# Score subtraction and exponential moved to the end of their own unit, and the last value product as one sum group

## The chip, the cores and the metric

The kernel runs on one core of a Trainium2 chip. The metric is the device time of one execution in microseconds (us); lower is better. Five runs of the kernel before the change stand behind its median, and one further run was taken with the hardware profiler.

## The reference

Two decode-attention blocks, A and B, each take one query token for 4 batch entries. Queries are `x @ wq` with 32 heads of 128, four query heads share one of 8 key/value heads, and the two results are concatenated:

```python
q = (x @ wq).reshape(B, 1, 32, 128).transpose(0, 2, 1, 3)
scores = einsum("bhqd,bhkd->bhqk", q, repeat(k, 4)) * 128 ** -0.5
o = einsum("bhqk,bhkd->bhqd", softmax(scores), repeat(v, 4))
out = o.reshape(B, 1, 4096) @ wo
```

Block A uses all 8192 keys of its cache; block B uses only the last 2048. Everything is bf16 at the interface. Nearly all bytes are keys and values: the profile counts 184.56 MB read.

## The kernel before, in words

**Units.** The work is cut into 20 units `u` of equal size (4 MB of keys, 4 MB of values). Units 0 to 3 are block B, one per batch entry with all 8 key/value heads; units 4 to 19 are block A, one per batch entry and pair of key/value heads. `L` is the last unit, 19. A unit has `NT` = 128 tiles of 128 keys. Two consecutive units make a *turn*; TensorE (PE) runs the ten turns as a hardware loop (`nc.Fori`), the other engines run straight code. Every engine's order is written out by hand: `op` and `add` append to one list per engine, and waits are named semaphore events such as `("exp", u)`.

**One unit on PE.** Sixteen jobs `T` transpose keys, eight tiles at a time, into one of four PSUM banks `KTB` (line 256). VectorE (DVE) copies the even jobs to SBUF (`ev[k]`, line 264), ScalarE (ACT) the odd ones (line 265). Three jobs later PE multiplies them with the queries (`pe_S`, line 289) into `SA[u % 2]` (first half of the scores) and `SB` (second half). Behind the sixteenth transpose, PE works on the unit before: `pe_SM(u-1)` sums its probabilities with a matrix of ones (line 315) and eight chunks `pe_PV(u-1, c)` of 16 matmuls multiply them with the values (line 303) into `OTB`, as `NSEG` = 4 sum groups of 32 tiles each. For block A the four groups are added later.

**One unit on the other engines.** At the end of unit `u`, DVE takes the maximum of the second half of its scores (`dve_max`, line 395; the first half's came earlier), joins the halves (`dve_maxc`), adds a mask (`dve_addmask`), and GpSimd (POOL) reduces the maximum over the partitions (`pool_ar1`, line 416, result `MB`). DVE then does the sum and reciprocal of unit `u-1` (`dve_sum`, `dve_rcp`) and `add_norm(u-1)`, which for block A adds the four groups (`OS`, line 469) and multiplies by the reciprocal (line 472). Only inside unit `u+1` does it treat unit `u`'s scores: after `ev[0]` the mask is taken off the maximum (`dve_submask`, line 423) and the first half of the scores is subtracted (`dve_sub`, line 433), after `ev[2]` the second half; ACT does the exponential (`act_exp`, line 442) after `ev[3]`, from `Dt` into `PT`.

**Output projection.** In the first unit of each turn three small jobs (`OT`, `OL`, `OPJ`) project the finished heads of one group; `OPJ` (line 366) needs a 1 MB piece of the output weight in `Wo_sb`. The last group is projected after the loop from `Wl_sb` (line 660).

**After the loop.** DVE and ACT do subtraction and exponential of unit `L`, PE seeds the two output banks (`pe_seed`, line 642), sums (`pe_SM(L)`), multiplies the eight value chunks into `KTB[0]`, whose loads arrive in four pieces (`VL`), and after `add_norm(L)` multiplies with the last weights; two copies and two small stores end the kernel.

**Loads.** All large loads are issued by SyncE (SP) in one order: keys of `u`, values of `u-1`, keys of `u+1`, and so on, with two buffers each. Keys of `u` wait for the last transpose of `u-2`, values of `u` for the last value product of `u-2`. The pieces of `Wo_sb` stand in the same queue, one per turn from turn 3 on.

Of the kernel before, what the change touches and what calls it, by code (L numbers as in the profile page):

```python
# [14 lines left out]
def bass_concat_heads__gqa_block_cached__sliding_block_cached__decode_kernel(  # L15
# [22 lines left out]
    NT = SK // 64  # L38
    NSEG = 4
    TS = NT // NSEG  # L40
    C = 2 * REP
# [9 lines left out]
    NW = 64  # L51
# [11 lines left out]
    L = NU - 1  # L63
# [6 lines left out]
    with ExitStack() as es:  # L70
# [30 lines left out]
        RL = sb("RL", [128, 4, NSEG * C], F32)  # L101
# [6 lines left out]
        PT = sb("PT", [128, 2, NT * C + NW], BF16)  # L108
        OT_sb = sb("OT_sb", [128, 2, NSEG, C, Bn], BF16)
# [21 lines left out]
        tjob_idx, qp_idx, xt_idx, perm_idx, ot_idx, ol_idx, opj_idx = {}, {}, {}, {}, {}, {}, {}  # L131
# [28 lines left out]
        def add(d):  # L160
            op(d["eng"], d["fn"], waits=d["waits"], inc=d["inc"])
# [132 lines left out]
        def pe_PV(u, c, bank=None, waits=()):  # L294
            otb = bank if bank is not None else OTB
            slot = u % 2

            def fn(pe):
                ins = None
                for i in range(TC):  # L300
                    t = c * TC + i
                    s, j = t // TS, t % TS
                    ins = pe.matmul(out=otb[:, s * NW:(s + 1) * NW], lhsT=V_sb[:, slot, t, :],  # L303
                                    rhs=PT[:, slot, t * C:t * C + NW], start=(j == 0), stop=(j == TS - 1))
                return ins
            op("pe", fn, waits=waits, inc=("PV", u * NC + c))

        def pe_SM(u):
            def fn(pe):
                ins = None  # L310
                for s in range(NSEG):
                    n = TS * C // NW
                    for i in range(n):
                        c0 = s * TS * C + i * NW
                        ins = pe.matmul(out=SA[u % 2][:, s * NW:(s + 1) * NW], lhsT=onesb[:, :], rhs=PT[:, u % 2, c0:c0 + NW],  # L315
                                        start=(i == 0), stop=(i == n - 1))
                return ins
            op("pe", fn, waits=[("exp", u) if u >= 0 else None], inc=("SM", u))
# [63 lines left out]
        def ncol(u):  # L382
            return NSEG * C if units[u]["P"] == 1 else C
# [35 lines left out]
        def dve_submask(u):  # L419
            n, P = ncol(u), units[u]["P"]  # L420

            def fn(dve):
                return dve.tensor_tensor(out=MBm[:, 0:n], in0=MB[:, 0:n], in1=MASK[P][:, 0:n], op=AluOpType.subtract)
            return dict(eng="dve", fn=fn, waits=[("ar1", u)], inc=("pm", u, 1))

        def dve_sub(u, h):
            S, n = nseg(u), ncol(u)
            Sh = max(1, S // 2)
            m0 = h * Sh * C if S > 1 else 0
            bank = SA[u % 2] if h == 0 else SB  # L430

            def fn(dve):
                return dve.tensor_tensor(  # L433
                    out=Dt[:, h * NTH * C:(h + 1) * NTH * C].rearrange("p (s j h) -> p s j h", s=Sh, h=C),
                    in0=bank[:, :].rearrange("p (s j h) -> p s j h", s=Sh, h=C),
                    in1=MBm[:, m0:m0 + Sh * C].rearrange("p (s o h) -> p s o h", o=1, h=C).broadcast_to([128, Sh, NTH // Sh, C]),
                    op=AluOpType.subtract)
            return dict(eng="dve", fn=fn, waits=[("pm", u, 1)], inc=("sub", u, h))

        def act_exp(u):  # L440
            def fn(act):
                return act.activation(out=PT[:, u % 2, 0:NT * C], in_=Dt[:, :], func=ACTF.Exp, scale=scale)  # L442
            return dict(eng="act", fn=fn, waits=[("sub", u, 1)] + ([("PV", (u - 2) * NC + NC - 1)] if u else []), inc=("exp", u))
# [10 lines left out]
        def dve_rcp(u):  # L454
            n = ncol(u)
            return dict(eng="dve", fn=lambda dve: dve.reciprocal(out=RL[:, u % 4, 0:n], in_=LB[:, 0:n]), waits=[("sum", u)], inc=("rcp", u))

        def add_norm(u, bank=None):
            un = units[u]
            P, b = un["P"], un["b"]  # L460
            otb = bank if bank is not None else OTB
            last = ("PV", u * NC + NC - 1)
            if P == 1:
                add(dict(eng="dve", fn=lambda dve: dve.tensor_tensor(
                    out=OT_sb[:, 1, :, :, b], in0=otb[:, 0:NSEG * NW].rearrange("p (g w) -> p g w", g=NSEG)[:, :, 0:C],
                    in1=RL[:, u % 4, :].rearrange("p (g c) -> p g c", g=NSEG), op=AluOpType.mult),
                    waits=[last, ("rcp", u)], inc=("otr", u)))
                return
            add(dict(eng="dve", fn=lambda dve: dve.tensor_reduce(
                out=OS[:, :], in_=otb[:, 0:NSEG * NW].rearrange("p (g w) -> p w g", g=NSEG)[:, 0:C, :], axis=AX.X, op=AluOpType.add),  # L470
                waits=[last] + ([("otr", u - 1)]), inc=("os", u)))
            add(dict(eng="dve", fn=lambda dve: dve.tensor_tensor(
                out=OT_sb[:, 0, un["gp"], :, b], in0=OS[:, :], in1=RL[:, u % 4, 0:C], op=AluOpType.mult),
                waits=[("os", u), ("rcp", u)], inc=("otr", u)))

        def dve_otp(tn):
            P, q = pieces.get(tn, (1, 0))
            w = [("pset",)]
            if tn in pieces:
                w.append(("otr", Bn - 1 if P == 1 else Bn + q * Bn + Bn - 1))  # L480
            if tn:
                w.append(("T", ot_idx[tn - 1]))
            return dict(eng="dve", fn=lambda dve: dve.tensor_copy(out=OTp[:, :, :], in_=OT_sb[:, P, q, :, :]), waits=w, inc=("otp", tn))

        def pool_setup0(pool):
# [87 lines left out]
        for u in range(NU):  # L573
            turn[0] = tn = u // 2
            odd = u % 2 == 0
            ev = {}
            extra = {}
            otp = dve_otp(tn) if odd else None
            at = -1

            def anchored(d):
                extra.setdefault(at, []).append(d)
            for tok in TOK:
                if tok[0] == "T":
                    ev[tok[1]] = pe_T(u, tok[1])
                    if tok[1] % 2 == 0:
                        at = tok[1]
                elif tok[0] == "S":
                    pe_S(u, tok[1])
                elif tok[0] == "SM":  # L590
                    pe_SM(u - 1)
                else:
                    pe_PV(u - 1, tok[1], waits=[("V", u - 1) if u >= 1 else None] if tok[1] == 0 else [])
                if odd and tok in AFTER:
                    kind = AFTER[tok][0]
                    anchored({"OT": pe_job_OT, "OL": pe_job_OL, "OPJ": pe_job_OPJ}[kind](tn))

            for k in range(0, NJ, 2):
                add(ev[k])
                if k == 0 and u >= 1:  # L600
                    add(dve_submask(u - 1))
                    add(dve_sub(u - 1, 0))
                if k == 2 and u >= 1:
                    add(dve_sub(u - 1, 1))
                if k == 2 and odd:
                    add(otp)
                if k == 10:
                    add(dve_max(u, 0))
                for d in extra.get(k, []):
                    add(d)  # L610
                    if "opj" in d:
                        follow[d["opj"]] = tjob_idx[(u, k + 2)]
            add(dve_max(u, 1))
            if units[u]["P"] == 0:
                add(dve_maxc(u))
            add(dve_addmask(u))
            if u >= 1:
                add(dve_sum(u - 1))
                add(dve_rcp(u - 1))
                add_norm(u - 1)  # L620

            for k in range(1, NJ, 2):
                add(ev[k])
                if k == 3 and u >= 1:
                    add(act_exp(u - 1))

            if u + 1 < NU:
                add(pool_rq(u + 1))
            add(pool_ar1(u))

        turn[0] = None
        add(dve_submask(L))
        add(dve_sub(L, 0))
        add(dve_sub(L, 1))
        add(act_exp(L))
        H2 = D // 2
        halves = [SA[(L + 1) % 2][0:Bn, 0:H2], KTB[2][0:Bn, 0:H2]]

# [3 lines left out]
                ins = pe.matmul(out=halves[hf], lhsT=identf[0:Bn, 0:Bn], rhs=oacc[:, 0, hf * H2:(hf + 1) * H2], start=True, stop=False)  # L642
            return ins
        op("pe", pe_seed, waits=[("ocp", NTURN - 1), ("otr", L - 1)])
        pe_SM(L)
        add(dve_sum(L))
        add(dve_rcp(L))
        VCH = [4, 2, 1, 1]
        vch_of = [i for i, n in enumerate(VCH) for _ in range(n)]
        for c in range(NC):  # L650
            w = [("VL", vch_of[c])]
            pe_PV(L, c, bank=KTB[0], waits=w)
        add_norm(L, bank=KTB[0])
        WCH = [3, 2, 2, 1]
# [46 lines left out]
        for u in range(1, NU + 1):  # L701
# [3 lines left out]
            tn = u // 2  # L705
# [174 lines left out]
```

## Time and profile before

| | us |
|---|---|
| median of 5 runs | 446.99 (445.70 to 447.89) |
| the profiled execution | 446.97 |
| its span in the profile | 445.2 |

| engine | busy us | share of the span |
|---|---|---|
| PE, matmuls | 365.2 | 82% |
| PE, weight loads | 333.3 | 75% |
| DVE | 208.6 | 47% |
| ACT | 181.7 | 41% |
| POOL | 21.3 | 5% |
| load queue, share of 16 DMA engines | | 97.7% |

A row of the timeline gives start, duration, engine, line, operation, tiles, count, and in brackets the idle time before it with what ended it. The chain of waits is followed backwards from the end of the kernel; each piece gives start, duration and place. Adjacent matmuls are merged, and their ends are modelled.

### The profile page before, as it was taken

The numbers are of one execution on the slowest core, as the hardware profiler recorded it, in microseconds if no ns is written. First come the engines' busy times: TensorE is split into PE (matmuls) and PEld (weight loads), VectorE is DVE, ScalarE is ACT, GpSimd is POOL, SyncE is SP. The second block draws the span as 40 slices with busy tenths as digits, with TensorE's granted clock in tenths as the row PEclk, the third lists the DMA queues.
The fourth block names the chain that finished last, engine by engine and source line by source line (L and its number), as shares of the span: only waits on it lengthen the run. The fifth ranks groups of instructions, "written<-read, shape, count | busy, mean of one in ns | idle before, by whom it ended". The sixth has DMA issues, their size and how long they took to land.

```text
span 445.2 us, 15658 instructions
## 1 busy us (share of the span) xinstructions
PE 365.2 (82%) x7282; PEld 333.3 (75%) x7282; DVE 208.6 (47%) x473; ACT 181.7 (41%) x183; POOL 21.3 (5%) x56
## 2 busy tenths in 40 slices
PE   0248897998998699679968988797799869977986
PEld 0248797898798589669956978597779749965985
DVE  0034265474564536455444546173636535553651
ACT  1004273463653518144533535252617333633541
POOL 6100000000000000000000000000000000000000
PEclk9999999999999999899988998899879978988999
DMA  8999999999999999999999999999999999999990
GB/s 342 417 416 422 419 417 420 423 443 414 443 425 439 430 427 434 427 427 433 436 426 431 430 430 420 441 434 436 424 424 433 433 427 433 434 407 445 428 386 29
DMA packets 13047, 184.78 MB, mean 415 GB/s; under 512 B 1332, under 2 KB 2408, under 8 KB 4456
## 3 DMA queue, kind: packets, MB, share of 16 engines
q1 hardware_dynamic: 12944, 184.56, 97.7%
q8 instruction: 8, 0.13, 0.1%
q14 instruction: 7, 0.06, 0.0%
q0 software_dynamic: 64, 0.02, 0.0%
q10 hardware_dynamic: 24, 0.01, 0.0%
HBM read 184.56 MB, written 0.01 MB: 415 GB/s over the span
## 4 chain that ended last, share of the span: by engine, by line
DMA 54%; PE 37%; DVE 4%; ACT 3%; issue 2%; SPq 1%
DMA Wo_sb<-in_B_wo_dram 27%; DMA Wo_sb<-in_A_wo_dram 20%; PE KT L256 11%; PE OT L303 11%; DMA K_sb<-in_B_k_cache_dram 7%; PE KT L366 6%; PE SB L289 4%; DVE Dt L433 2%; PE SA L315 2%; DVE KT_sb L264 1%; ACT PT L442 1%; PE SA L289 1%; SPq L537 1%; ACT KT_sb L265 1%; PE KT L303 1%
## 5 line engine op out<-in xcount | busy, mean ns | idle before, releaser
L265 ACT ACTIVATE KT_sb<-KT 128x1024 bf16<-128x1024 bf16 x160 | 160.9, 1021 | 226.1 <-PE KT L256 225.8
L256 PE MATMUL KT<-identf,K_sb 128*128 128x128 f32 x1280 | 204.7, 294 | 32.6 <-DMA K_sb<-in_A_k_cache_dram 19.6
L256 PEld LDWEIGHTS KT<-identf,K_sb 128*128 128x128 f32 x1280 | 145.5, 148 | 42.6 <-DMA K_sb<-in_A_k_cache_dram 20.6
L264 DVE COPY KT_sb<-KT 128x512 int32<-128x512 int32 x160 | 110.2, 688 | 89.6 <-PE KT L256 88.1
L303 PE MATMUL OT<-PT,V_sb 128*128 128x64 bf16 x2560 | 84.4, 193 | 1.6 <-issue 1.5
L303 PEld LDWEIGHTS OT<-PT,V_sb 128*128 128x128 bf16 x2560 | 78.4, 98 | 1.8 <-issue 1.6
L289 PEld LDWEIGHTS SA<-RQc,KT_sb 128*128 128x128 bf16 x1280 | 55.5, 97 | 5.3 <-ACT KT_sb L265 3.3
L289 PE MATMUL SA<-RQc,KT_sb 128*128 128x16 bf16 x1280 | 56.1, 170 | 1.0
L289 PE MATMUL SB<-RQc,KT_sb 128*128 128x16 bf16 x1280 | 55.9, 170 | 0.0
L289 PEld LDWEIGHTS SB<-RQc,KT_sb 128*128 128x128 bf16 x1280 | 52.3, 97 | 1.4
L366 PE MATMUL KT<-Wo_sb,OL 128*4 128x512 bf16 x80 | 26.8, 497 | 18.4 <-DMA Wo_sb<-in_B_wo_dram 10.5
L395 DVE TENSOR_REDUCE M<-SB 128x8 f32<-128x512 f32 (+1 forms) x20 | 13.8, 692 | 43.4 <-PE SB L289 43.4
L366 PEld LDWEIGHTS KT<-Wo_sb,OL 128*4 128x4 bf16 x80 | 7.4, 100 | 31.5 <-issue 27.2
L416 POOL PARTITION_ALL_REDUCE MB<-M1m x20 | 7.7, 385 | 394.1 <-DVE M1m L409 394.1
L442 ACT ACTIVATE PT<-Dt 128x1024 bf16<-128x1024 f32 x20 | 21.1, 1056 | 10.7 <-DVE Dt L433 10.7
L187 PE MATMUL KT<-ident,x_sb 4*128 4x4 bf16 x8 | 0.6, 170 | 18.9 <-POOL identf L499 18.9
L187 PEld LDWEIGHTS KT<-ident,x_sb 4*128 4x128 bf16 x8 | 0.4, 112 | 19.1 <-issue 19.1
L433 DVE TENSOR_TENSOR Dt<-SA,MBm 128x512 f32<-128x512 f32 x20 | 13.8, 691 | 0.7
L315 PE MATMUL SA<-PT,onesb 128*128 128x64 bf16 x336 | 13.2, 192 | 0.7 <-ACT PT L442 0.7
L395 DVE TENSOR_REDUCE M<-SA 128x8 f32<-128x512 f32 (+1 forms) x20 | 13.6, 681 | 0.0
L433 DVE TENSOR_TENSOR Dt<-SB,MBm 128x512 f32<-128x512 f32 x20 | 13.6, 681 | 0.0
L315 PEld LDWEIGHTS SA<-PT,onesb 128*128 128x128 bf16 x336 | 11.1, 97 | 1.2 <-ACT PT L442 1.2
(68 smaller groups left out, 110.9 us busy)
## 6 DMA issues: line engine op xcount, KB each, us to landing
K_sb<-in_A_k_cache_dram SPq DMA_DIRECT2D x16, 4096.0 KB, 24.1
V_sb<-in_A_v_cache_dram SPq DMA_DIRECT2D x15, 4096.0 KB, 29.1
K_sb<-in_B_k_cache_dram SPq DMA_DIRECT2D x16, 1024.0 KB, 22.1
V_sb<-in_B_v_cache_dram SPq DMA_DIRECT2D x16, 1024.0 KB, 20.3
V_sb<-in_B_wq_dram SPq DMA_DIRECT2D x1, 4096.0 KB, 12.5
V_sb<-in_A_wq_dram SPq DMA_DIRECT2D x1, 4096.0 KB, 21.9
Wo_sb<-in_B_wo_dram SPq DMA_DIRECT2D x4, 1024.0 KB, 30.8
Wo_sb<-in_A_wo_dram SPq DMA_DIRECT2D x3, 1024.0 KB, 29.8
```

The source lines that it names most:

```text
L256: ins = pe.transpose(out=bkf[:, pi * 128:(pi + 1) * 128], in_=K_sbf[:, slot, t0:t0 + 2, :].rearrange("p t d -> p (t d)"), identity=identf[ ...
L264: return e.tensor_copy(out=KT_sb.bitcast(I32)[:, tj % NKT, :], in_=bkf.bitcast(I32)[:, :])
L265: return e.activation(out=KT_sb[:, tj % NKT, :], in_=bk[:, :], func=ACTF.Copy)
L289: ins = pe.matmul(out=stb[:, t % NTH * C:(t % NTH + 2) * C], lhsT=ktv[:, pi, :, e], rhs=RQc[:, u % 2, t // TS, e, :], start=(e == 0), stop ...
L303: ins = pe.matmul(out=otb[:, s * NW:(s + 1) * NW], lhsT=V_sb[:, slot, t, :], rhs=PT[:, slot, t * C:t * C + NW], start=(j == 0), stop=(j == ...
L315: ins = pe.matmul(out=SA[u % 2][:, s * NW:(s + 1) * NW], lhsT=onesb[:, :], rhs=PT[:, u % 2, c0:c0 + NW], start=(i == 0), stop=(i == n - 1))
L366: ins = pe.matmul(out=bk[0:Bn, 0:D], lhsT=OL[:, i // REP, i % REP, :], rhs=Wo_sb[:, i // REP, i % REP, :], start=(i == 0), stop=(i == C - 1))
L395: return dve.tensor_reduce(out=M1[:, h * n:(h + 1) * n].rearrange("p (s h) -> p s h", h=C), in_=bank[:, :].rearrange("p (s j h) -> p s h j ...
L416: return pool.partition_all_reduce(MB[:, 0:n], M1m[:, 0:n], channels=128, reduce_op=ReduceOp.max)
L433: return dve.tensor_tensor(out=Dt[:, h * NTH * C:(h + 1) * NTH * C].rearrange("p (s j h) -> p s j h", s=Sh, h=C), in0=bank[:, :].rearrange ...
L442: return act.activation(out=PT[:, u % 2, 0:NT * C], in_=Dt[:, :], func=ACTF.Exp, scale=scale)
L537: return e.dma_start(out=dst, in_=src)
```

## The change

Every unit's `dve_submask`, both `dve_sub` and `act_exp` are moved from the following unit to the end of their own: on DVE they stand between `dve_rcp(u-1)` and `add_norm(u-1)`, before the next unit's `ev[0]`; on ACT the exponential stands behind `ev[15]`, before the next unit's `ev[1]`. For the last unit the same happens inside the loop over units rather than after it. After the loop, `pe_SM(L)` is placed behind the fourth of the eight value chunks, the first value chunk waits for the exponential, all 128 matmuls of the last value product form one sum group, and the last `add_norm` is a single multiplication from PSUM. `dve_otp` gets one more wait, for the latest multiplication of `add_norm`.

```diff
@@ pe_PV
-                    s, j = t // TS, t % TS
+                    n = TS if bank is None else NT
+                    s, j = t // n, t % n
                     ins = pe.matmul(out=otb[:, s * NW:(s + 1) * NW], lhsT=V_sb[:, slot, t, :],
-                                    rhs=PT[:, slot, t * C:t * C + NW], start=(j == 0), stop=(j == TS - 1))
+                                    rhs=PT[:, slot, t * C:t * C + NW], start=(j == 0), stop=(j == n - 1))
@@ add_norm
+            if bank is not None:
+                add(dict(eng="dve", fn=lambda dve: dve.tensor_tensor(
+                    out=OT_sb[:, 0, un["gp"], :, b], in0=otb[:, 0:C], in1=RL[:, u % 4, 0:C], op=AluOpType.mult),
+                    waits=[last, ("rcp", u)], inc=("otr", u)))
+                return
@@ dve_otp
-                w.append(("T", ot_idx[tn - 1]))
+                w += [("T", ot_idx[tn - 1]), ("otr", 2 * tn - 2)]
@@ the loop over units
                 add(ev[k])
-                if k == 0 and u >= 1:
-                    add(dve_submask(u - 1))
-                    add(dve_sub(u - 1, 0))
-                if k == 2 and u >= 1:
-                    add(dve_sub(u - 1, 1))
...
             if u >= 1:
                 add(dve_sum(u - 1))
                 add(dve_rcp(u - 1))
+            add(dve_submask(u))
+            add(dve_sub(u, 0))
+            add(dve_sub(u, 1))
+            if u >= 1:
                 add_norm(u - 1)
 
             for k in range(1, NJ, 2):
                 add(ev[k])
-                if k == 3 and u >= 1:
-                    add(act_exp(u - 1))
+            add(act_exp(u))
@@ after the loop
-        add(dve_submask(L))
-        add(dve_sub(L, 0))
-        add(dve_sub(L, 1))
-        add(act_exp(L))
...
-        pe_SM(L)
         add(dve_sum(L))
         add(dve_rcp(L))
...
             w = [("VL", vch_of[c])]
+            if c == 0:
+                w.append(("exp", L))
+            if c == 4:
+                pe_SM(L)
             pe_PV(L, c, bank=KTB[0], waits=w)
```

## The prediction

> **What bounds the kernel now.** I read the queue table first, then the chain of waits, then the timeline around its last pieces.
>
> ```profile
> q1 hardware_dynamic: 12944, 184.56, 97.7%
> ```
>
> ```profile
> 376.60 29.78 DMA Wo_sb<-in_A_wo_dram
> 406.51 2.99 PE KT L366 x8
> ...
> 417.59 0.48 PE KT L256 x4
> 418.10 0.69 DVE KT_sb L264
> 418.90 0.69 DVE Dt L433
> 419.59 0.59 DVE KT_sb L264
> 420.19 0.61 DVE Dt L433
> 420.82 1.06 ACT PT L442
> 421.88 0.92 ACT KT_sb L265
> ...
> 433.30 1.30 DVE Dt L433 x2
> 434.62 1.06 ACT PT L442
> 435.73 0.64 PE SA L315 x16
> 436.37 3.75 PE KT L303 x128
> ```
>
> The loads fill the DMA engines to 97.7% of the span. The last weight piece is issued at 376.60 and lands 29.78 us later, behind queued keys and values. So until 406.4 the kernel is as fast as the loads, and issuing one a microsecond sooner or later changes nothing. From 406.5 PE never waits for a load again (the DMA share falls to 0.56 in 433 to 436 us). The chain from there is compute: the rest of unit 18, unit 19, then subtraction, exponential, sums, values, projection. Only these 39 us can be won or lost by reordering engines.
>
> Two places in them carry the work that is moved. Inside unit 19 the exponential (420.82) holds up ACT's copy of job 5 (421.78), and PE's scores of job 5 start at 422.84 instead of about 422.48. After the loop everything waits for the exponential at 434.62. The DVE timeline shows why it is that late:
>
> ```profile
> 430.91 0.17 DVE L409 TENSOR_TENSOR M1m<-M1c,MASKA 128x8 f32<-128x8 f32 x1
> 432.80 0.19 DVE L469 TENSOR_REDUCE OS<-OT 128x8 f32<-128x32 f32 x1 [1.15 <-PE OT L303]
> 433.02 0.18 DVE L472 TENSOR_TENSOR OT_sb<-OS,RL 128x8 bf16<-128x8 f32 x1
> 433.11 0.16 DVE L423 TENSOR_TENSOR MBm<-MB,MASKA 128x8 f32<-128x8 f32 x1
> ```
>
> DVE idles 1.15 us for the value product of unit 18 before it normalizes and only then subtracts, though the reduced maximum may have been there long before:
>
> ```profile
> 431.17 0.37 POOL L416 PARTITION_ALL_REDUCE MB<-M1m  x1 [14.79 <-DVE M1m L409]
> ```
>
> **The change part by part.** *Before 406.4.* The moves add no instruction and issue no DMA; SP's and POOL's orders stay. What they delay or hasten is covered by the load queue: in unit 18 PE waits 2.82 us for keys and 2.28 us for the weight. Were that cover gone, each boundary would cost or yield the tenths worked out next.
>
> *Boundary 18 to 19.* DVE before: reciprocal 416.28 to 416.48, idle, normalization 417.63 to 418.04, `ev[0]` at 418.10. After: `dve_submask` at 416.51, subtractions at 416.70 and 417.30 (the pitch of 433.30/433.90), done 417.98; normalization from 417.91, `ev[0]` at 418.23, done 418.92. PE's four transposes last until 419.1 anyway, so scores of job 0 start at 419.10 as before. On ACT the exponential runs 418.01 to 419.07 and `ev[1]` ends at 419.99 (pitch 0.96 as at 420.82/421.78): scores of job 1 start at 420.03, not 419.78, a loss of 0.25. In return no exponential stands between `ev[3]` and `ev[5]`, and job 5 comes at 420.03 + 4 x 0.675 = 422.73 against 422.84. Unit 19 ends 0.11 earlier.
>
> *Tail.* Shifted by -0.11, DVE's reciprocal ends at 431.53, then mask and two subtractions to 433.03, exponential 433.06 to 434.12 (before: 435.68). But PE is not free then:
>
> ```profile
> 433.97 0.59 PE L642 MATMUL SA<-oacc,identf 4*4 4x256 f32 x2 [1.21 <-DVE OT_sb L472]
> 434.40 0.59 PE L642 MATMUL KT<-oacc,identf 4*4 4x256 f32 x2
> ```
>
> The seed starts 0.77 after the multiplication that it waits for has ended, and 1.2 after the last loop matmul; other turn ends show the same pause with nothing late (1.28 at 71.16, 1.21 at 106.36). I take it as the loop's own, so moving the normalization 0.35 later behind the subtractions costs nothing, and the seed occupies PE until 434.40 + 0.43 = 434.83, less 0.11 = 434.72. The value product starts there instead of 435.73: 0.90 from the tail itself. The sixteen sums (0.48) keep their price behind chunk 4; sum and reciprocal then end near 437.9, before the last value matmul at 439.1. Value pieces: the last pair, issued by 418.9 with 16.4 to landing, is there by 435.3, needed at 438.6. One sum group instead of four alters flags only: 29.3 ns a matmul in the tail, 29.5 in the loop, whose groups are 32 long; cost nothing. The last `OS` goes, 440.14 to 440.37; the multiplication now reads PSUM, between 0.18 (L472) and 0.23 (L464, 128x32). I take a gain of 0.22. Line 660's weights have stopped moving by 438.0, before 439.5, when they are needed.
>
> *Waits added.* `dve_otp` waits for a multiplication two copies earlier on its own engine: nothing. The first value chunk waits for the exponential, with the whole tail behind it: priced above. `dve_submask` waits for POOL with subtractions, normalization and the next unit's copies behind it. POOL's row ends at 431.54, against 431.64 when DVE gets there; the next POOL copy starts 0.24 to 0.34 after each such row's start. The lower bound is thus no wait. The upper: before, the consumer at 433.11 follows its predecessor by 0.09, without a stop, so the result was there, at most 1.57 after the row's end, 1.44 beyond DVE's arrival. The Trainium skill speaks against the change here: "GPSIMD Engine Reference", section "3.2 Cross-partition — where GPSIMD wins", measures a partition-axis `tensor_reduce` of [128, 2048] at 247,699 ns, 121 ns a column, an estimate of 0.97 us for 8 columns: 0.47 of wait. But this is another instruction, and here 32 columns take 0.43 and 8 take 0.37. I go by the row: no wait.
>
> *The clock.* With the exponential out of the way PE reaches `OPJ` of unit 18 some 0.55 sooner (the 0.51 wait at 400.40 goes) and idles about 2.85 instead of 2.28 for the weight, which lands when it did. Idle time makes `OPJ` slow:
>
> ```profile
> 197.43 1.89 PE L366 MATMUL KT<-Wo_sb,OL 128*4 128x512 bf16 x8 [2.03 <-DMA Wo_sb<-in_B_wo_dram]
> 406.51 2.99 PE L366 MATMUL KT<-Wo_sb,OL 128*4 128x512 bf16 x8 [2.28 <-DMA Wo_sb<-in_A_wo_dram]
> 322.66 3.57 PE L366 MATMUL KT<-Wo_sb,OL 128*4 128x512 bf16 x8 [2.61 <-DMA Wo_sb<-in_A_wo_dram]
> 364.06 3.57 PE L366 MATMUL KT<-Wo_sb,OL 128*4 128x512 bf16 x8 [3.08 <-DMA Wo_sb<-in_A_wo_dram]
> ```
>
> The granted clock is 0.71 in 405 to 410 us. The two other rows (3.10 and 3.27 idle) took 3.22 and 3.36. The four rows at 2.6 to 3.3 idle average 3.43, 0.44 over the 2.99. "TensorE: Matmul & The Clock Gate", section "HAM oscillation — how this bites in real kernels", only warns of gaps above about 3.4 us, so by it 2.85 costs nothing. The rows show a price from 2.06 on; I take +0.44, with ends of 0 and +1.1 (turn 8, whose next transposes were slow too), and below nothing -1.1 if it falls as at 197.43.
>
> *Sum.* -0.11 - 0.90 - 0.22 = -1.23; with the clock -0.79. Against the profiled 446.97 (span 445.2 and 1.77 around it; the median, 446.99, is the same) that is 446.2. By the page's clock rule it would be 445.7; by its reduction price, working through the formula of the second rival, 446.8.
>
> **The rivals.** *The clock is kind.* The gate does not fall further, or `OPJ` comes out as at 197.43: -1.23 to -2.3, 444.7 to 445.7. For it: 2.03 and 2.06 idle gave 1.89 and 2.58, so phase matters. Against: four of four rows above 2.6 are slow.
>
> *POOL is late.* The all-reduce really ends x after DVE wants it. At the boundary normalization and both first copies move by x; at the tail the exponential by x again, less 0.33 that the seed hides. Total -0.79 + x + (x - 0.33): even at x = 0.56, and past +1.34 from x = 1.23; the bound of 1.44 gives +1.8, 448.7. For it: POOL's rows are rough, and nothing before tested them. Against: the copies that start behind them.
>
> *PE's code after the loop is not there in time.* A 1.51 "issue" gap stands in the first pass of the value product (53.63). Before, PE's wait for the exponential (0.75) could hide such a gap: up to +1.5, so 447.7, more with a cold clock. Against: nothing of the kind in the tail before.
>
> *Nothing changes.* Excluded as far as order goes: the exponential can't stay at 434.62 unless POOL is late.
>
> **How the numbers follow.** A measurement of this kernel can tell about 0.3%, 1.34 us, from no change. Forecast 0.40 (own range 445.0 to 447.2; faster 0.14, same 0.24, slower 0.02). Kind clock 0.28 (0.23, 0.05, 0). Late POOL 0.22 (0, 0.10, 0.12). Late code 0.10 (0, 0.06, 0.04). Together faster 0.37, same 0.45, slower 0.18. The range leaves out one in ten on each side, the lowest of the kind clock and the highest of late POOL: 444.7 to 448.3.
>
> **What would show it.** Right: `Dt` and `PT` rows ahead of the next unit's first copies; `dve_submask` within 0.1 of the reciprocal's end; in unit 19 no ACT stop near job 5; after the loop value matmuls directly behind the seed, no `OS` row. Wrong: idle before `dve_submask` on POOL's `MB`, a pause between seed and values, or the last weight not landing near 406.4, which would mean that loads moved after all. The length of `OPJ` and of the transposes behind it decides the clock term.

## The result and the profile after

The changed kernel takes 445.73 us in the median of 42 runs, the kernel before 447.37 in 79: ratio 0.9961, 95% interval 0.9950 to 0.9972, or 1.7 us less (1.25 to 2.2 by the interval). Here and below the ratio on record, not the quotient of the two medians, is what a comparison is judged by; the two can differ by 0.2%. The profiled execution took 444.37 (span 442.6), one of the shortest. The times of both kernels are spread over several us: 444.2 to 447.8 after, 445.3 to 450.4 before. The experiments below trace a large part of that spread to the clock of TensorE.

The chain of waits of the changed kernel from its last load on (start, duration, what):

```profile
385.26 30.82 DMA K_sb<-in_A_k_cache_dram
416.12 1.97 PE KT L256 x16
...
428.42 0.70 DVE M L396
430.25 0.57 issue
430.82 0.45 DVE Dt L434
431.82 0.59 issue
432.41 0.59 PE SA L642 x2
433.00 0.43 PE KT L642 x2
433.43 1.97 PE KT L304 x64
435.40 0.47 PE SA L316 x16
435.87 1.88 PE KT L304 x64
```

Two things are new. The last wait for a load is no longer the weight piece of unit 18 but the keys of unit 19, which land at 416.1; TensorE gets there too early and waits 0.24 for them. And no exponential stands in the tail: the value product follows the seed directly. DVE's and POOL's rows show the moved work where it was put:

```profile
429.88 0.20 DVE L457 RECIPROCAL RL<-LB 128x8 f32<-128x8 f32 x1
430.01 0.17 DVE L424 TENSOR_TENSOR MBm<-MB,MASKA 128x8 f32<-128x8 f32 x1
430.21 0.69 DVE L434 TENSOR_TENSOR Dt<-SA,MBm 128x512 f32<-128x512 f32 x1
```

```profile
429.61 0.37 POOL L417 PARTITION_ALL_REDUCE MB<-M1m  x1 [14.83 <-DVE M1m L410]
```

The mask is taken off 0.13 after the reciprocal's start, with no wait for POOL. The chain after the loads splits at four marks: the projection `OPJ` of unit 18, the first transposes of unit 19, the maximum of its second half (line 396, 395 before), and the first matmul with the last weights. The table gives them for every kernel: the start and the duration of `OPJ`, then differences of start times in the timelines.

| kernel | `OPJ` starts | `OPJ` lasts | `OPJ` to unit 19 | unit 19 to maximum | maximum to last weights |
|---|---|---|---|---|---|
| before | 406.51 | 2.99 | 10.92 | 12.55 | 10.71 |
| changed | 406.50 | 1.89 | 9.62 | 12.30 | 9.68 |
| tail_only | 406.88 | 1.89 | 9.61 | 12.58 | 9.64 |
| loop_only | 406.29 | 2.73 | 10.87 | 12.36 | 13.44 |
| warm_before | 407.52 | 1.89 | 9.44 | 12.57 | 11.99 |
| warm_after | 406.89 | 1.89 | 9.41 | 12.31 | 11.19 |
| tail_fill_before | 406.20 | 1.89 | 9.63 | 12.58 | 10.71 |
| seed_late | 406.27 | 2.70 | 10.88 | 12.36 | 10.10 |
| seed_late_warm | 406.19 | 1.89 | 9.73 | 12.30 | 10.09 |
| late_more | 406.35 | 3.40 | 10.97 | 13.58 | 11.98 |
| fixed_before | 406.31 | 1.89 | 9.74 | 12.57 | 10.72 |
| seed_late_warm2 | 406.41 | 1.89 | 9.71 | 12.30 | 10.09 |

Between the two profiled executions the tail gives 1.03, unit 19 gives 0.25, and the stage of the projection 1.30, together the 2.6 between the spans (445.2 and 442.6). The first two repeat in every kernel whose clock is undisturbed there: 12.3 or 12.6 in unit 19 by the loop's order, 9.64 to 9.68 or 10.71 behind it by the tail's order. These 1.28 us are what the change does. The 1.30 are not: `OPJ` ran at full clock in one execution and not in the other.

```profile
406.50 1.89 PE L367 MATMUL KT<-Wo_sb,OL 128*4 128x512 bf16 x8 [2.52 <-DMA Wo_sb<-in_A_wo_dram]
```

The comparison of many runs gave 1.7, and 1.28 lies just inside its interval. So something beyond the fixed part may differ on average too. The experiments look for it.

### The profile page after: what moved, and what is told of

It reads as the page before. It is cut to its first block, busy times and chain, and to the rows that moved or that the text cites. A ratio compares the mean times of both kernels' runs of the same rounds, so it can differ in the third digit from the quotient of the medians.

```text
span 442.6 us, 15650 instructions
## 1 busy us (share of the span) xinstructions
PE 363.4 (82%) x7282; PEld 332.4 (75%) x7282; DVE 210.2 (47%) x472; ACT 184.0 (42%) x183; POOL 21.3 (5%) x56
## 4 chain that ended last, share of the span: by engine, by line
DMA 54%; PE 42%; issue 2%; SPq 1%; DVE 1%; ACT 0%
DMA Wo_sb<-in_B_wo_dram 27%; PE KT L256 17%; DMA Wo_sb<-in_A_wo_dram 13%; PE OT L304 10%; DMA K_sb<-in_A_k_cache_dram 7%; DMA K_sb<-in_B_k_cache_dram 7%; PE KT L367 6%; PE SB L289 4%; PE SA L289 2%; PE SA L316 1%; SPq L543 1%; PE KT L304 1%; PE SA L663 0%; PE KT L663 0%; DVE M L396 0%
## 5 line engine op out<-in xcount | busy, mean ns | idle before, releaser
L379 DVE TENSOR_TENSOR oacc<-KT,oacc 4x512 f32<-4x512 f32 x4 | 2.7, 678 | 24.1 <-PE KT L367 24.1
```

## The experiments

**One half of the change each.**

`tail_only` keeps the order of before for units 0 to 18:

```diff
+                if k == 0 and u >= 1:
+                    add(dve_submask(u - 1))
+                    add(dve_sub(u - 1, 0))
+                if k == 2 and u >= 1:
+                    add(dve_sub(u - 1, 1))
...
-            add(dve_submask(u)); add(dve_sub(u, 0)); add(dve_sub(u, 1))
+            if u == L:
+                add(dve_submask(u)); add(dve_sub(u, 0)); add(dve_sub(u, 1))
...
+                if k == 3 and u >= 1:
+                    add(act_exp(u - 1))
-            add(act_exp(u))
+            if u == L:
+                add(act_exp(u))
```

> The order of the kernel before for units 0 to 18, and the changed order, sum group and normalization for the last unit only. Theory A (fixed gain of 1.28 us: 1.03 after the loop, 0.25 inside unit 19; what is over that is the clock of TensorE around the projection of unit 18): 1.0 us below before, ratio about 0.9977; from the start of the last unit's second-half maximum to the first matmul with the last weights 9.7 us as in the changed kernel (10.7 before). Rival B (the order inside the loop brings most of it, since TensorE runs ahead and loads follow): 0.3 us or less below before, 0.9993 or more.

Measured: 446.11 against 447.65, ratio 0.9977 (0.9952 to 1.0001); the tail 9.64, unit 19 12.58. Both stages and the ratio are those of theory A, but the interval still holds 1.

`loop_only` is its mirror (`if u < L` in both places, everything after the loop as before).

> The changed order for units 0 to 18; subtraction, exponential, sums, values and normalization of the last unit as before. Theory A: 0.25 us from unit 19, give or take the clock lottery of some 0.5: ratio 0.9985 to 1.0005; from the second-half maximum of the last unit to the first matmul with the last weights 10.7 us as before, from the first transpose of unit 19 to that maximum 12.3 (12.55 before). Rival B: 1.2 to 1.5 us below before, 0.997.

Measured: 447.21 against 447.65, ratio 1.0010 (0.9993 to 1.0027); unit 19 12.36. Rival B falls: the order inside the loop brings nothing that this comparison can measure, and the 1.2 to 1.5 that it asked for lie outside the interval. But one expectation failed. The tail, which should have been the 10.7 of before, took 13.44 in the profiled execution, which was the longest of the twelve runs (449.92). TensorE's rows of `loop_only` behind its loop:

```profile
435.28 1.03 PE L316 MATMUL SA<-PT,onesb 128*128 128x64 bf16 x16 [0.78 <-ACT PT L443]
436.12 6.25 PE L304 MATMUL KT<-PT,V_sb 128*128 128x64 bf16 x128
```

The same 16 and 128 matmuls took 0.64 and 3.90 in the kernel before, whose tail this is. The table by stretches names the reason; its columns are the stretch, its length, busy time of PE, PEld, DVE, ACT and POOL with counts, the granted clock (1.00 is TensorE's full clock), DMA share and GB/s. First `loop_only`, then the kernel before:

```profile
434.00:436.00 2.00, 1.22 (x17) 0.72 (x15) 0.13 (x1) 1.06 (x1) 0.00 (x0) 0.62 0.34 122
436.00:438.00 2.00, 2.00 (x42) 2.00 (x40) 0.63 (x2) 0.00 (x0) 0.00 (x0) 0.50 0.09 29
```

```profile
434.00:436.00 2.00, 1.25 (x13) 0.48 (x14) 0.58 (x1) 1.06 (x1) 0.00 (x0) 1.00 0.38 135
436.00:438.00 2.00, 2.00 (x75) 2.00 (x72) 0.63 (x2) 0.00 (x0) 0.00 (x0) 1.00 0.10 31
```

At equal work the granted clock is 0.50 in one execution and 1.00 in the other. So there are two places where a weakly used TensorE may lose its clock: `OPJ`, after the wait for the weight, and the value product behind the loop.

**The first place.** 32 idle matmuls before `OPJ`, in both kernels (`warm_before`, `warm_after`):

```diff
+            def wfn(pe):
+                ins = None
+                for i in range(32):
+                    ins = pe.matmul(out=bk[:, 0:128], lhsT=onesb[:, :], rhs=ident[:, :], start=True, stop=True)
+                return ins
+            op("pe", wfn, waits=[("E", ol_idx[tn]), bankfree(idx)])
```

> The kernel before, and 32 idle matmuls (128x128, ones times identity, into the bank that the projection then overwrites) ahead of the projection in each turn, so that TensorE idles some 0.5 us for the weight piece, not 2.3. Clock theory: the eight projection matmuls take 1.9 us in the last turn, unit 19 starts when its keys have landed (about 416.1), and the runs gather at the lowest times of the kernel before: median near 445.6, 1.7 below before, ratio 0.996. Rival C (the spread of the runs comes from the loads, not from the clock): no change, 1.0, or 1 to 2 us slower by the added matmuls where TensorE does not wait.

Measured: 446.67 against 447.65, ratio 0.9990 (0.9968 to 1.0012).

> The changed kernel with the same 32 idle matmuls. Clock theory: median near 444.4, ratio to before 0.9934; the difference to the kernel before with the idle matmuls is the fixed gain alone, 1.2 to 1.3 us. Rival C: as the changed kernel, 0.996, or slower.

Measured: 445.73, ratio 0.9961 (0.9940 to 0.9983).

`OPJ` takes 1.89 us in the last turn of both, as the clock theory says. The medians did not fall as far as it says, and the two profiled executions show two reasons: the idle matmuls end after the weight has landed, so `OPJ` starts at 407.52 and 406.89 instead of 406.5, and the tail lost its clock in both (11.99 and 11.19). The rows of `warm_after`:

```profile
405.01 1.95 PE L373 MATMUL KT<-ident,onesb 128*128 128x128 bf16 x32
406.89 1.89 PE L367 MATMUL KT<-Wo_sb,OL 128*4 128x512 bf16 x8
...
433.51 3.12 PE L304 MATMUL KT<-PT,V_sb 128*128 128x64 bf16 x64
```

**The second place.** `tail_fill_before` is the kernel before, with seven idle matmuls on each side of the seed, inside TensorE's wait for the exponential:

```diff
+        filler(7)
         op("pe", pe_seed, waits=[("ocp", NTURN - 1), ("otr", L - 1)])
+        filler(7)
```

where `filler(n)` multiplies ones with the identity n times into a bank that nothing reads any more.

> The kernel before with seven idle matmuls (128x128) on each side of the seed, in the wait of TensorE for the exponential of the last unit, 0.8 us of work that ends before the exponential does. Theory D (a second clock lottery: between the loop's end and the last value product TensorE does almost nothing for 3.0 us before and 2.2 after the change, and the value product then runs in 3.75 us or in up to 6.1): the value product stays near 3.75, ratio 0.997 to 0.999, no run slower for it. Rival E (the slow value product has nothing to do with what precedes it): ratio 1.000, and value products over 4.5 us still occur.

Measured: 445.97 against 447.77, ratio 0.9968 (0.9944 to 0.9992). Fourteen matmuls whose result nobody uses bring 1.4 us (0.4 to 2.5), with the tail at the same 10.71 as in the profile before. They take no work off the path and start nothing sooner: the exponential still releases the sums. That no run would be slow was expected and missed: four of the twelve took 446.9 to 448.3. None of these four was profiled in detail, so whether they lost the time in `OPJ` or in the tail is not shown.

```profile
433.70 0.56 PE L648 MATMUL KT<-ident,onesb 128*128 128x128 bf16 x7
434.17 0.64 PE L315 MATMUL SA<-PT,onesb 128*128 128x64 bf16 x16
434.64 3.90 PE L303 MATMUL KT<-PT,V_sb 128*128 128x64 bf16 x128
```

The change shortens the same stretch, unasked: between the loop's last value matmuls and the next full ones, TensorE has only the small seed for 2.96 us before (432.77 to 435.73) and for 2.16 us after (431.20 to 433.36).

`seed_late` takes the change one step further and puts the seed behind the fourth value chunk:

```diff
-        op("pe", pe_seed, waits=[("ocp", NTURN - 1), ("otr", L - 1)])
...
             if c == 4:
+                op("pe", pe_seed, waits=[("ocp", NTURN - 1), ("otr", L - 1)])
                 pe_SM(L)
```

> The changed kernel with the seed of the output banks behind the fourth value chunk, so that full matmuls follow the loop's end at once. Without any effect of the clock 0.1 to 0.25 us slower than the changed kernel, since the value product waits for the exponential by itself (ratio to before 0.9965). Theory D: idle time ahead of the value product falls from 2.2 to 1.4 us, the slow value product becomes rare, median 0.3 to 0.7 below the changed kernel, ratio 0.995 or less.

Measured: 445.42, ratio 0.9952 (0.9929 to 0.9974). The weak stretch is 1.54 us, the value chunks ran at full clock (2.03 for 64), and the tail is 10.10, 0.42 longer than in the changed kernel (0.1 to 0.25 was expected). That the median is nevertheless not higher agrees with theory D; against the changed kernel alone the intervals overlap. The spans say it more clearly: in seven of these twelve runs the device time is 2.3 to 2.9 above the span instead of about 1.8, and the median span is 443.05 against 443.8 for the changed kernel (44 runs, not side by side). Such time outside the span, 2.2 to 3.1 in 13 of 82 runs of the kernel before, is a part of the spread of run times that lies ahead of the first or behind the last instruction.

`seed_late_warm` adds 16 idle matmuls, half as many as before, so that they end ahead of the weight:

> As the run with the late seed, and 16 idle matmuls ahead of the projection in each turn (0.95 us of a wait of 2.5). Both clock theories: projection 1.9 us, unit 19 starts at about 416.1, value product 3.8 us: runs gather at 444.4 to 445.2, ratio 0.9935 to 0.995. If the idle time that is left (1.5 us) is enough for the clock to fall, no better than the late seed alone.

Measured: 444.74 against 447.77, ratio 0.9934 (0.9904 to 0.9964), runs from 444.45 to 444.83. The changed kernel varied by 3.5 us over 42 runs; this one varies by 0.4 over seven, and both places show full clock:

```profile
406.19 1.89 PE L367 MATMUL KT<-Wo_sb,OL 128*4 128x512 bf16 x8 [0.86 <-DMA Wo_sb<-in_A_wo_dram]
...
432.53 2.03 PE L304 MATMUL KT<-PT,V_sb 128*128 128x64 bf16 x64 [1.54 <-ACT PT L449]
```

**Both remedies without the change, and once more with it.** `fixed_before` is the kernel before with the 16 and the 7 + 7 idle matmuls; `seed_late_warm2` repeats the last kernel.

> The kernel before, its order unchanged, with both groups of idle matmuls: 16 ahead of the projection in each turn and seven on each side of the seed. If the clock is all that sets runs apart, they gather within some 0.5 us at the lowest times of the kernel before, 445.4 to 445.8, ratio 0.9955 or less, although nothing of the change is in it. The difference to the changed kernel with idle matmuls and late seed is then the order's fixed gain alone: 1.28 less the 0.4 that the late seed costs, 0.9. If the order matters beyond that, the difference is 1.5 or more, or the runs stay spread over 2 us.

Measured: 446.04 against 447.38, ratio 0.9975 (0.9951 to 0.9999). Eight of the twelve runs lie between 445.4 and 446.4, four between 447.1 and 447.8: the idle matmuls help the old order, but do not secure it. Its tail still has a gap of 1.1 us and the seed between them; that the four lost their time there is likely, not shown, since the profiled execution is one of the eight (445.61). Expected was a narrow set of runs; that was missed.

> The changed kernel with 16 idle matmuls and the late seed once more, beside the kernel before with its idle matmuls on the same chip: again 444.4 to 444.9 and a spread under 0.5 us, ratio 0.993 to 0.995, if the first result was not a lucky set of runs.

Measured: 444.86, ratio 0.9938 (0.9918 to 0.9959), runs from 444.54 to 445.38. The first result was no luck. This version beats the kernel before. It is also below the changed kernel, at 444.7 to 444.9 against 445.7 in the median, and all its 19 runs are under that 445.7; but the two were compared only by way of the kernel before, and those intervals overlap. The lowest runs of `fixed_before` and of this kernel are 445.41 and 444.54, 0.87 apart, where 1.28 less 0.42 for the late seed gives 0.86. This fits an order that is worth what the stages say when the clock is out of play; the medians, with the four long runs in them, are 1.18 apart.

**POOL late on purpose.** `late_more` delays the all-reduce of the last two units:

```diff
+                if u >= L - 1:
+                    pool.memset(scr[:, 0:1400], 0.0)
                 return pool.partition_all_reduce(MB[:, 0:n], M1m[:, 0:n], channels=128, reduce_op=ReduceOp.max)
```

> The changed kernel with a 1400-column memset (about 1.24 us) on GpSimd ahead of the all-reduce of units 18 and 19 only. DVE then waits about 1.1 us before the mask is taken off. By the prediction's formula 1.1 + 0.8 = 1.9 us are lost between the projection of unit 18 and the end, apart from clock effects; with the slack seen in the changed trace (first ACT copy of unit 19 ready 0.15 before it is needed, exponential done 0.7 before the seed) 1.0 in unit 19 and 0.6 behind it. Rival: the wait is hidden behind TensorE's value product and under 0.5 is lost.

Measured: 449.01 us, one execution. The wait is there, in both units:

```profile
417.51 0.17 DVE L427 TENSOR_TENSOR MBm<-MB,MASKA 128x8 f32<-128x8 f32 x1 [1.14 <-POOL MB L420]
...
433.70 0.17 DVE L427 TENSOR_TENSOR MBm<-MB,MASKA 128x8 f32<-128x8 f32 x1 [1.13 <-POOL MB L420]
...
435.64 0.59 PE L645 MATMUL SA<-oacc,identf 4*4 4x256 f32 x2 [1.96 <-DVE OT_sb L481]
```

Unit 19 takes 13.58 instead of 12.30, and from its maximum to the first value matmul it is 5.69 (430.90 to 436.59) instead of 4.94 (428.42 to 433.36). That is 1.28 + 0.75 = 2.03 us, near the 1.9 of the formula; the rival of a hidden wait is out. The formula's second part was right in size but not in its way: the exponential ends at 436.28, and the value product waits for the seed, which the late normalization holds up. The rest of its time over the changed kernel is clock: `OPJ` took 3.40, and the first 64 value matmuls 3.06.

## Why the prediction was right, and what was wrong in it

*Bound by loads until 406.4: right.* `OPJ` starts at 406.50 after and 406.51 before, though the weight was issued 1.0 earlier (375.61). "PE never waits for a load again" was wrong for the changed kernel: with a fast `OPJ` the keys of unit 19 are the last wait, 416.12. In this execution that is a floor: TensorE can't gain more than about 1.3 in unit 18.

*Unit 19: -0.11 predicted, -0.25 measured.* The stop at job 5 went, as said. The loss of 0.25 at job 1 did not come, because in this execution TensorE started the unit 0.28 later after the maximum of unit 18 (2.90 instead of 2.62), on its keys, while DVE and ACT kept their pace:

```profile
416.34 1.06 ACT L443 ACTIVATE PT<-Dt 128x1024 bf16<-128x1024 f32 x1 [4.28 <-DVE Dt L434]
417.30 1.92 ACT L265 ACTIVATE KT_sb<-KT 128x1024 bf16<-128x1024 bf16 x2
```

In `loop_only`, where the keys are not late, job 1 lost 0.07 (scores 2.53 after the first transpose instead of 2.46) and unit 19 took 12.36, a gain of 0.19. So the term of job 1 was too large there as well.

*Tail: -0.90 and -0.22 predicted, -1.03 measured for both.* The pause of 1.2 after the loop is its own, as assumed: the seed starts 1.21 after the last loop matmul again, now 0.60 after the multiplication it waits for, not 0.77. The seed, not the exponential, releases the value product. The difference of 0.09 lies in 0.09 between seed and first value matmul, which the sum had at nothing. The vanished `OS` gave 0.22: from the last value matmul to the first with the last weights it is 0.35 (437.75 to 438.10) instead of 0.57. The rows of the seed and of the last multiplication:

```profile
432.41 0.59 PE L642 MATMUL SA<-oacc,identf 4*4 4x256 f32 x2 [1.21 <-DVE OT_sb L478]
437.77 0.18 DVE L471 TENSOR_TENSOR OT_sb<-KT,RL 128x8 bf16<-128x8 f32 x1 [1.21 <-PE KT L304]
```

The rival of late code did not show: no pause like the 1.51 at 53.63 stands between seed and value product.

*POOL: right.* No wait, and the row's end can be trusted at this size: the all-reduce of 0.37 held DVE neither in unit 18 nor in unit 19, where the mask is taken off 0.03 after that end. The price of a partition-axis reduction from the Trainium skill ("GPSIMD Engine Reference", section "3.2 Cross-partition — where GPSIMD wins"), 0.97 by the prediction's estimate, would have left 0.47 of idle time there, and there is none. What a late POOL would have cost, `late_more` confirms in the total (2.03 for 1.93 by the formula with x = 1.13).

*The clock: the step that failed.* The term was +0.44, from rows that show `OPJ` slower after more idle time. Its rows were right as far as they went: in the changed profile the six other turns idle 2.6 to 4.1 us and take 2.95 to 3.57. But the last turn took 1.89, the "kind clock" rival. TensorE reached `OPJ` only 0.25 sooner, not 0.55, and idled 2.52, not 2.85. Above all the idle time alone does not set the price: over the seven profiles without idle matmuls ahead of it, the last `OPJ` took 3.40 after 1.50, 2.99 after 2.28, 1.89 after 2.46, 2.52 and 2.53, and 2.70 and 2.73 after 2.61 and 2.63. First `tail_only`, then `late_more`:

```profile
406.88 1.89 PE L367 MATMUL KT<-Wo_sb,OL 128*4 128x512 bf16 x8 [2.46 <-DMA Wo_sb<-in_A_wo_dram]
406.35 3.40 PE L368 MATMUL KT<-Wo_sb,OL 128*4 128x512 bf16 x8 [1.50 <-DMA Wo_sb<-in_A_wo_dram]
```

The traces show what stands in its place. In all twelve the granted clock changes only at marks 3.41 us apart, whose place differs from execution to execution, and each of the 106 complete stretches at half clock is 3.41 or 6.83 us long. The kernel before had a mark at 407.14, with 1.13 of TensorE work in the 3.41 us ahead of it, and its clock fell there, inside `OPJ`. The changed execution had one at 408.23, with 1.73 of work ahead of it, nearly all of `OPJ`, and kept its clock. The columns are those of the table by stretches; first before, then changed:

```profile
403.73:407.14 3.41, 1.13 (x14) 0.68 (x13) 0.96 (x2) 1.05 (x2) 0.00 (x0) 1.00 1.04 448
407.14:410.56 3.42, 3.42 (x17) 1.58 (x16) 0.68 (x1) 0.00 (x0) 0.00 (x0) 0.50 0.96 412
```

```profile
404.82:408.23 3.41, 1.73 (x8) 0.62 (x8) 0.00 (x0) 0.04 (x1) 0.00 (x0) 1.00 1.04 449
408.23:411.64 3.41, 3.41 (x71) 3.28 (x71) 1.97 (x3) 1.62 (x2) 0.00 (x0) 1.00 1.00 432
```

So the 1.89 of the changed profile goes with where its marks lay, and two kernels with the old order inside the loop show the same 1.89.

The term also looked at one place only. The second, the value product behind the loop, was not in the sum at all, though the change shortens just that weak stretch by 0.80. Filling the stretch brings the kernel before 1.4 us on average by `tail_fill_before` (0.4 to 2.5). That a smaller loss there makes up what the 1.7 have over the fixed 1.28 is the reading I hold for likely, not one that was shown; by the interval there may be next to nothing to make up. How those 0.4 divide between the two places is open: `loop_only` is compatible with a slower `OPJ`, as predicted, and the intervals of half a per cent are too wide to say. The rule that the Trainium skill gives in "TensorE: Matmul & The Clock Gate", section "HAM oscillation — how this bites in real kernels", warns only of gaps above about 3.4 us; it does not cover this kernel, where a pause of 1.2 and a seed of 0.95 were enough in `warm_after`, and 1.50 of idle time ahead of `OPJ` in `late_more`.

The forecast time, 446.2, is 0.5 above the median measured, because it adds 0.44 for the clock to a fixed part of -1.23 that was right (-1.28); beyond the fixed part the runs show no loss, and by the ratio a gain of 0.4. The 445.7 that the prediction gave by the page's clock rule meets the median, but by luck: `OPJ` did run slow after gaps far below 3.4 us, and the tail's clock was in neither sum. A gain of 1.7 is past the prediction's own limit of 1.34, the outcome "faster" to which it gave 0.37, less than the 0.45 for "same".

## What to carry to other kernels

When runs of one kernel spread over more than the effect to be judged, split the profile into stages and compare them one by one before believing a total: here 1.28 of the 2.6 us between two profiles were fixed, and the other half was the clock of one stage. A reordering that shortens a stretch in which TensorE does almost nothing may gain twice, by the wait and by the clock of what follows; a handful of idle matmuls in a wait tests that cheaply, if they end before the awaited data come. Work that is early only moves the wait to the next load, so look when that one lands.

## What was not expected of the hardware

After 1.1 to 1.2 us without matmuls and 0.95 us of two small matmuls (4 rows, 256 columns, f32), the granted clock fell in some executions: in `warm_after` 64 value matmuls took 3.12 us instead of 2.03, and in `loop_only`, where a wait of 0.78 follows the seed, the clock was 0.50 and 128 took 6.25 instead of 3.90. With 1.54 us of pause and full matmuls behind it (`seed_late` and its two companions) three of three profiles stayed at full clock, and the times of the two that also have idle matmuls ahead of `OPJ` narrowed to 0.4 and 0.8 us.

That the clock falls in some executions of a kernel and not in others goes with the marks 3.41 us apart. I split the twelve traces at their marks from 44 us on and took the stretches at full clock. All 92 with less than 1.50 us of TensorE work were followed by half clock, none of the 1056 with more than 2.23 were, and of the 97 between, 14. Two tails lie almost alike between their marks; first `loop_only`, whose clock fell, then the kernel before, whose clock stayed:

```profile
431.08:434.49 3.41, 2.23 (x46) 1.37 (x42) 1.83 (x6) 0.32 (x1) 0.00 (x0) 1.00 0.96 331
431.04:434.45 3.41, 2.20 (x62) 1.84 (x59) 2.16 (x8) 0.00 (x0) 0.37 (x1) 1.00 0.97 337
```

The busy time is the same, but the seed makes up 1.01 of it in the first and 0.48 in the second; without it they are 1.22 and 1.72. So the small seed seems to count for little or nothing; no run tested it apart from the length of the pause. An estimate from these rows: if some 1.5 us of full work are needed between two marks, a weak stretch may cover 1.9 of the 3.41. The 2.96 before the change then cost the clock at about three in ten places of the marks, the 2.16 after it at fewer than one in ten, and 1.54 at none. A fall cost 1.3 to 2.7 us in the profiled tails of `warm_before`, `warm_after` and `loop_only`.
